# Loads of the start phase: all of X first, two weight tiles from ScalarE's queue, one split ahead of the lead, seven banks in turn

## The chip, the cores and the metric

The kernel runs on one core of one Trainium2 chip. The metric is the device time of one execution in microseconds. Five engines work side by side, each through its own instructions in order, and wait for each other by semaphores: TensorE (PE in the profile, its weight loads PEld), VectorE (DVE), ScalarE (ACT), GpSimd (POOL) and SyncE (SP). SP, ACT and POOL also issue the DMA transfers. The rows SPq and ACTq are those engines' queues: a DMA that stands there waiting holds up whatever stands behind it on the same engine.

## The reference

For x of 2048 rows and 576 columns there are two attentions of 32 heads of 18 columns each, one with its own keys and values per head (A) and one in which all heads share a key and a value (B), mixed by a gate.

```python
g = _sigmoid((x * gate_w).sum(-1, keepdims=True))
a = _A_ref(x, A_wqkv, A_wo)              # 32 heads: softmax(q k^T / sqrt(18)) v, then @ wo
b = _B_ref(x, B_wq, B_wk, B_wv, B_wo)    # the same, one k and one v for all heads
return g * a + (1 - g) * b
```

Everything is float32. The kernel forms most products from a rounded high part and a low part (h and l), three products of halves for each product.

## The kernel before

X is held transposed: 576 rows (the contraction, in five slabs of 128 with the last half full twice) by 2048 columns. All projection weights stand side by side in `wall`, cut into 14 tiles of 128 columns. Tile 0 holds B's shared key, the gate, B's shared value and the first queries. Tiles 0 to 4 are projected at the start and in the lead, the other nine later, in between the attention's own work.

The work runs in three stretches.

1. **The start phase** (to about 50 us). Tiles 0, 1 and 2 are projected for the four chunks of 512 columns of X. X's first chunk comes as two halves (`xsh`), the others as `xs`, numbered 2, 3 and 4 in the code's `load_x`. Each load is three DMAs: the main part of 128 partitions by `load5`, then the last 64 rows twice. Each chunk is cut into halves by `split_x`: ACT makes the high part `xh` (line 388), DVE the low part `xl` (394) and the last slab's low part (398). PE does 14 products per tile and chunk (line 278). `leave` takes the bank out of PSUM: ACT writes the high part of `phl` (284) and, for tile 0, a plain copy `pst` (287); DVE makes the low part (289); DMAs store them (`kq`, `qk`). `shared_v` then turns the value rows of `pst` round on PE (line 326), so PE waits there for ACT's copy. PE's order is fixed by the code: after tile 0 and tile 1 of the first chunk stand the four transposes of line 326, then tile 2, then the second chunk.
2. **The lead** (to about 91 us), whose order is written out as a string of letters. A and B are half-height products of tiles 3 and 4 (line 963), x and y are the first heads' score maxima (1115), taken out by ACT (1119, `xd`) and DVE (1125, `junk`).
3. **The main stretch**, in which scores, exponentials, maxima and the second products of all 64 heads alternate, ordered by strings and a small clock model. PE sets its pace to the end.

Banks of PSUM: seven are given out. In the start phase `Clock.turn` hands them out in fixed rings, ring "s" of three for projections and ring "m" of four for the warming products and `shared_v`. From the lead on, the bank that the model frees first is taken.

Queues: SP issues nearly all loads and the small stores of `kq`, ACT four loads at the very beginning, POOL a few loads and the large stores. The DMAs of SP and ACT share eight completion semaphores, called DMAHW0 to DMAHW7 in the built program, handed out in turn. Before a DMA takes a semaphore, its earlier user must have landed, and the issuing engine waits for that. `load_x(4)`, the last chunk of X, and the weights of tiles 3 and 4 are issued on SP behind the stores of the first chunk. Tile 3 is split (`prep_w`, lines 250 and 251) in the start phase, tile 4 inside the lead.

Of the kernel before, what the change touches and what calls it, by code (L numbers as in the profile page):

```python
# [8 lines left out]
F32 = mybir.dt.float32  # L9
# [19 lines left out]
NT = 5  # L29
# [18 lines left out]
class Clock:  # L48


    def __init__(self):
        self.free = [0.0] * 7
        self.t = self.act = self.dve = self.last = 0.0
        self.mode, self.begun, self.tail = "", [0.0, 0.0], [0.0, 0.0]
        self.turns, self.count, self.held, self.diffs, self.copies = {"s": 0, "m": 0}, 0, {}, [], []
        self.cleared, self.half = 0.0, HALF_MM

    def turn(self, which):
        n = self.turns[which]
        self.turns[which] += 1  # L60
        self.count += 1
        k = n % 3 if which == "s" else 3 + n % 4
        self.free[k] = -1e6 + self.count
        return k

# [91 lines left out]
def gated_mix_kernel(ctx: ExitStack, tc: tile.TileContext, xT, wall, wv, wo, out):  # L157
    nc = tc.nc
    P = 128

    def dma(o, i, eng=None):
        o, i = (x.bitcast(F32) if x.dtype == F32R else x for x in (o, i))
        return (eng or nc.sync).dma_start(o, i)  # L163
# [46 lines left out]
    def in_turn(which):  # L210
        return bank_tile(clk.turn(which))
# [24 lines left out]
    def split(src, h, l, eng_h, eng_l):  # L236
        if eng_h is nc.scalar:
            nc.scalar.activation(h, src, AF.Copy)
        else:
            eng_h.tensor_copy(h, src)  # L240
        if l is not None:
            eng_l.tensor_tensor(l, src, h.bitcast(F32), op=OP.subtract)

    def load5(t, src, rest=None):
        dma(t[:, 0:4, :], src[0:512, :].rearrange("(p k) m -> p k m", p=P))
        dma(t[0:64, 4, :], src[512:576, :], rest)
        dma(t[64:128, 4, :], src[512:576, :], rest)

# [1 line left out]
        nc.scalar.activation(w["h"], st, AF.Copy)  # L250
        eng_l.tensor_tensor(w["l"], st, w["h"].bitcast(F32), op=OP.subtract)

    def load_w(mt, rest=None):
        st = wpool.tile([P, NKT, P], F32, name="wst", bufs=5)
        load5(st, wall[mt], rest)
        return st

    def prep_w(st):
        w = {y: wpool.tile([P, NKT, P], F32R, name=f"w{y}", bufs=3) for y in "hl"}
        split_w(st, w, nc.vector)  # L260
        return w
# [4 lines left out]
    def project(mt, c, w, parts=1):  # L266


        fp = in_turn("s")
        g = 512 // parts  # L270
        for i in range(parts):
            products(fp, w, c * 512, g * i, g)
        return leave(mt, c, fp)
# [47 lines left out]
        return c, st  # L321

    def shared_v(c, st):
        pv = in_turn("m")
        for j in range(4):
            nc.tensor.transpose(pv[:, 18 * j:18 * j + 18],
                                st[ROW_VB:ROW_VB + 18, j * P:(j + 1) * P],
                                ident[ROW_VB:ROW_VB + 18, ROW_VB:ROW_VB + 18])
        nc.vector.tensor_copy(vb[:, 4 * c:4 * c + 4, 0:18],
                              pv[:, 0:72].rearrange("p (j d) -> p j d", d=18))  # L330
# [35 lines left out]
    with tc.tile_pool(name="xs", bufs=1, side="right") as xsp:  # L366
        XS = []

        def load_x(c, rest=None):
            half = c < 2  # L370
            XS.append(xsp.tile([P, NKT, 256 if half else 512], F32, name="xsh" if half else "xs", bufs=2 if half else 3))
            load5(XS[c], xT[:, 256 * c:256 * c + 256] if half else xT[:, 512 * (c - 1):512 * c], rest)

        def main_w(st):

            w = {y: wpool.tile([P, NKT, P], F32R, name=f"w{y}", bufs=3) for y in "hl"}
            nc.scalar.activation(w["h"][:, 0:4], st[:, 0:4], AF.Copy)
            nc.vector.tensor_tensor(w["l"][:, 0:4], st[:, 0:4], w["h"][:, 0:4].bitcast(F32), op=OP.subtract)
            return w

        def last_w(st, w):
            nc.scalar.activation(w["h"][:, 4], st[:, 4], AF.Copy)
            nc.vector.tensor_tensor(w["l"][:, 4], st[:, 4], w["h"][:, 4].bitcast(F32), op=OP.subtract)

        def split_x(c):
            xs = XS[c // 2 + 1][:, :, 256 * (c % 2):256 * (c % 2) + 256] if c > 1 else XS[c]
            cs = slice(c * 256, (c + 1) * 256)
            nc.scalar.activation(X["h"][:, :, cs], xs, AF.Copy)
            low_x(c, xs)
            last_x(c, xs)  # L390

        def low_x(c, xs):
            cs = slice(c * 256, (c + 1) * 256)
            nc.vector.tensor_tensor(X["l"][:, :, cs], xs[:, 0:4], X["h"][:, 0:4, cs].bitcast(F32), op=OP.subtract)

        def last_x(c, xs):
            xh = X["h"][64:128, 4, c * 256:(c + 1) * 256]
            nc.vector.tensor_tensor(xh, xs[64:128, 4], xh.bitcast(F32), op=OP.subtract)

        W = [load_w(0, nc.scalar)]  # L400
        load_x(0, nc.scalar)
        nc.scalar.activation(ones, ones, AF.Copy)
        W.append(load_w(1, nc.gpsimd))
        W.append(load_w(2, nc.gpsimd))
        load_x(1, nc.gpsimd)

        warm = in_turn("m")
        for i in range(6):
            nc.tensor.matmul(warm[:, 0:304], ident, vb.rearrange("p k d -> p (k d)"), start=True, stop=True)
        for c in range(2, 4):  # L410
            load_x(c)
        dma(ones_r.rearrange("a (b c) -> (a b) c", c=32), ones)

        x0, xh = XS[0], X["h"][:, :, 0:256]
        ST = [W.pop(0) for _ in range(3)]
        WP = [main_w(ST[0])]
        nc.scalar.activation(xh[:, 0:2], x0[:, 0:2], AF.Copy)
        nc.vector.tensor_copy(xh[:, 2:4], x0[:, 2:4])
        low_x(0, x0)
        WP.append(main_w(ST[1]))  # L420
        WP.append(main_w(ST[2]))
        last_w(ST[0], WP[0])
        nc.scalar.activation(xh[:, 4], x0[:, 4], AF.Copy)
        last_x(0, x0)
        last_w(ST[1], WP[1])
        last_w(ST[2], WP[2])
        split_x(1)
        FP = [in_turn("s") for _ in range(3)]
        for n in ((0, 12), (12, 14)):
            for mt in range(3):  # L430
                products(FP[mt], WP[mt], 0, 0, 256, *n)
        keep = []

        def chunk(c):
            split_x(2 * c)
            split_x(2 * c + 1)

        for mt in range(3):
            if mt == 2:
                chunk(1)  # L440
                shared_v(*keep.pop())
            products(FP[mt], WP[mt], 0, 256, 256)
            keep.append(leave(mt, 0, FP[mt]))
            keep = [k for k in keep if k]
            if mt == 0:
                load_x(4)
                for m in range(3, NT):
                    W.append(load_w(m))
        for n, (mt, c) in enumerate(FIRST):
            if n == 1:  # L450
                chunk(2)
            if n == 2:
                chunk(3)
            if keep and keep[0][0] <= n - 2:
                shared_v(*keep.pop(0)[1])
            done = project(mt, c, WP[mt], 2 if n == 0 else 1)
            if done:
                keep.append((n, done))
            if (mt, c) == (0, 2):
                first_back()  # L460
            if (mt, c) == (0, 3):
                rows_back()
            if n == 6:
                WP.append(prep_w(W.pop(0)))

    xdp = ph1.enter_context(tc.tile_pool(name="xdp", bufs=1, side="right"))
    small = ctx.enter_context(tc.tile_pool(name="small", bufs=1, side="left"))
# [619 lines left out]

    def lead_units():
        yield
        for mt in range(3, NT):  # L1090
            w = WP.pop()
            for c in range(4):
                if (mt, c) == (3, 1):
                    for _ in range(NT - 4):
                        WP.append(prep_w(W.pop(0)))
                st = stp.tile([P, 512], F32, name="pst", bufs=3)
                st2 = xdp.tile([P, 512], F32, name="pst2", bufs=2)

                def done(mt=mt, c=c, st=st, st2=st2):
                    hl = stp.tile([P, 2, 512], F32R, name="phl", bufs=4)  # L1100
                    nc.gpsimd.tensor_tensor(st, st, st2, op=OP.add)
                    split(st, hl[:, 0, :], hl[:, 1, :], nc.gpsimd, nc.gpsimd)
                    dma(qk_d[:, mt * P:(mt + 1) * P, c * 512:(c + 1) * 512].rearrange("a p f -> p a f"), hl,
                        nc.gpsimd)

                yield Unit([(w[a][:, k, :], X[b][:, k, c * 512:(c + 1) * 512]) for a, b, k, _ in PROJ],
                           512, (st, st2), done, how="both", upper=-1)

    def lead_max(what, low):
        M, h = pairs[what].pop(0)  # L1110
# [187 lines left out]
```

## Time and profile before

| what | value |
|---|---|
| median of three runs | 2636.14 us (2635.72 to 2636.35) |
| the profiled execution, its own time | 2633.82 us |
| its span, first to last instruction | 2632.0 us |
| PE busy | 2621.7 us, 100% of the span |
| ACT busy, DVE busy | 2447.6 us and 2395.4 us |
| granted TensorE clock, mean | 0.999 |
| start phase, PE's products of line 278 | 7.81 to 50.5 us |

A row of the timeline gives the start in us, the duration, the engine, the line, the operation with output<-input, the number of instructions merged, and in brackets the idle time before it and what ended that. The chain of work that ended last gives start, duration and the work or transfer that held the end. PE's busy time is modelled and says little about how full it is; the chain and the gaps say more.

### The profile page before, as it was taken

The numbers are of one execution on the slowest core, as the hardware profiler recorded it, in microseconds if no ns is written. First come the engines' busy times: TensorE is split into PE (matmuls) and PEld (weight loads), VectorE is DVE, ScalarE is ACT, GpSimd is POOL, SyncE is SP. The second block draws the span as 40 slices with busy tenths as digits, with TensorE's granted clock in tenths as the row PEclk, the third lists the DMA queues.
The fourth block names the chain that finished last, engine by engine and source line by source line (L and its number), as shares of the span: only waits on it lengthen the run. The fifth ranks groups of instructions, "written<-read, shape, count | busy, mean of one in ns | idle before, by whom it ended". The sixth has DMA issues, their size and how long they took to land.

```text
span 2632.0 us, 66889 instructions
## 1 busy us (share of the span) xinstructions
PE 2621.7 (100%) x25213; PEld 1404.5 (53%) x25213; DVE 2395.4 (91%) x4575; ACT 2447.6 (93%) x4862; POOL 850.5 (32%) x1087
## 2 busy tenths in 40 slices
PE   9999999999999999999999999999999999999999
PEld 7655545545455455554554555545555544545665
DVE  6899999999999999999999999999998999999883
ACT  5999999999999999999999999999999999999887
POOL 3611000211364535644554446443310020012113
PEclk9999999999999999999999999999999999999999
DMA  8412112212343234323544344434432332234312
GB/s 259 140 54 62 36 48 59 75 48 74 96 123 105 91 97 120 113 89 93 152 130 137 119 138 141 142 118 121 141 95 76 101 98 85 61 88 126 110 56 92
DMA packets 176328, 270.28 MB, mean 103 GB/s; under 512 B 58905, under 2 KB 137193, under 8 KB 164625
## 3 DMA queue, kind: packets, MB, share of 16 engines
q1 hardware_dynamic: 159813, 212.70, 28.2%
q0 software_dynamic: 15152, 51.79, 5.3%
q8 instruction: 198, 3.24, 0.5%
q10 hardware_dynamic: 1040, 1.52, 0.2%
q14 instruction: 125, 1.02, 0.1%
HBM read 190.26 MB, written 66.90 MB: 98 GB/s over the span
## 4 chain that ended last, share of the span: by engine, by line
PE 98%; DMA 1%; DVE 0%; ACT 0%; SPq 0%; POOL 0%; issue 0%; ACTq 0%; DVEq 0%
PE acc L755 39%; PE bank L695 29%; PE bank L740 17%; PE bank L963 11%; PE bank L278 1%; PE bank L1115 0%; PE bank L943 0%; DMA xsh<-xT 0%; PE acc L767 0%; DMA R<-r_d 0%; SPq L163 0%; POOL oacc L936 0%; DMA wst<-wall 0%; PE bank L1017 0%; DMA sm<-sum_d 0%
## 5 line engine op out<-in xcount | busy, mean ns | idle before, releaser
L748 ACT ACTIVATE pt<-bank 128x512 f32<-128x512 f32 x4096 | 2146.4, 616 | 120.4 <-PE bank L740 68.7
L704 DVE TENSOR_REDUCE mx<-bank 128x1 f32<-128x512 f32 x3002 | 1886.9, 684 | 118.2 <-PE bank L740 60.3
L740 PE MATMUL bank<-qs,ksb 56*128 56x512 f32 x2688 | 906.8, 424 | 0.0
L695 PE MATMUL bank<-ksb,qs 54*128 54x512 f32 x2270 | 806.4, 426 | 0.0
L755 PE MATMUL acc<-pt,vb 128*19 128x256 f32 (+3 forms) x6144 | 553.2, 455 | 0.0
L695 PEld LDWEIGHTS bank<-ksb,qs 54*128 54x128 f32 x2270 | 382.8, 184 | 318.8 <-ACT pt L748 190.3
L755 PE MATMUL acc<-pt,vg 128*19 128x512 f32 (+3 forms) x5952 | 535.0, 455 | 0.0
L740 PEld LDWEIGHTS bank<-qs,ksb 56*128 56x128 f32 x2688 | 441.1, 184 | 153.9 <-DVE mx L704 63.8
L740 PE MATMUL bank<-qs,ksa 56*128 56x512 f32 x1408 | 466.6, 425 | 0.0
L695 PE MATMUL bank<-ksa,qs 54*128 54x512 f32 x1232 | 439.2, 426 | 0.0
L701 DVE CUSTOM_DVE_ANT_0 junk<-bank,xb 128x512 bf16<-128x512 f32 x500 | 342.9, 686 | 29.4 <-PE bank L740 23.6
L698 ACT ACTIVATE xb<-bank 128x512 f32<-128x512 f32 x500 | 292.6, 606 | 13.7 <-PE bank L740 3.2
L695 PEld LDWEIGHTS bank<-ksa,qs 54*128 54x128 f32 x1232 | 207.8, 184 | 151.1 <-ACT pt L748 87.4
L240 POOL CAST mh<-mt 128x32 fp32r<-128x32 f32 x62 | 13.0, 210 | 831.1 <-DVE mt L713 608.8
L740 PEld LDWEIGHTS bank<-qs,ksa 56*128 56x128 f32 x1408 | 225.5, 184 | 84.2 <-DVE mx L704 31.3
L755 PEld LDWEIGHTS acc<-pt,vb 128*19 128x19 f32 x6144 | 123.1, 97 | 203.1 <-issue 169.6
L755 PEld LDWEIGHTS acc<-pt,vg 128*19 128x19 f32 x5952 | 119.7, 97 | 206.2 <-issue 180.2
L240 POOL CAST rhl<-rst 128x292 fp32r<-128x292 f32 (+2 forms) x81 | 34.0, 420 | 486.7 <-issue 316.4
L963 PE MATMUL bank<-xr,wrh 64*128 64x292 f32 (+1 forms) x1134 | 167.9, 300 | 0.0
L695 PE MATMUL bank<-kdb,qs 54*128 54x512 f32 x372 | 159.8, 430 | 0.0
L963 PEld LDWEIGHTS bank<-xr,wrh 64*128 64x128 f32 x1134 | 139.5, 186 | 2.8
L558 POOL TENSOR_TENSOR xr<-xst,xr 128x876 fp32r<-128x876 f32 (+1 forms) x63 | 130.4, 2070 | 0.0
(171 smaller groups left out, 2397.0 us busy)
## 6 DMA issues: line engine op xcount, KB each, us to landing
qs<-qk SPq DMA_DIRECT2D x366, 144.0 KB
xst<-xT SPq DMA_DIRECT2D x54, 438.0 KB
ksa<-qk SPq DMA_DIRECT2D x132, 144.0 KB
qk<-rhl POOLq DMA_DIRECT2D x54, 292.0 KB, 4.3
ksb<-qk SPq DMA_DIRECT2D x60, 144.0 KB
qk<-phl POOLq DMA_DIRECT2D x16, 512.0 KB, 5.4
onh<-oh POOLq DMA_DIRECT2D x32, 256.0 KB, 3.9
onl<-ol POOLq DMA_DIRECT2D x32, 256.0 KB, 4.7
```

What stands on the lines that cost most here:

```text
L240: eng_h.tensor_copy(h, src)
L278: nc.tensor.matmul(fp[:, p0:p0 + g], w[a][:kr, k, :], X[b][:kr, k, x0 + p0:x0 + p0 + g], start=(n == 0), stop=(n == len(PROJ) - 1))
L558: nc.gpsimd.tensor_tensor(x[:, 5:8, 0:n], t0, x[:, 0:3, 0:n].bitcast(F32), op=OP.subtract)
L695: nc.tensor.matmul(pm, qs[u % 3][b:b + 54, i * P:(i + 1) * P], k, start=True, stop=True)
L698: nc.scalar.activation(MX["x", u, i], pm, AF.Relu)
L701: nc.vector.tensor_tensor_reduce(junk, pm, MX.pop(("x", u, i)), 1.0, -3e38, op0=OP.add, op1=OP.max, accum_out=MX[u][:, i, c:c + 1])
L704: nc.vector.tensor_reduce(MX[u][:, i, c:c + 1], pm, axis=AX.X, op=OP.max)
L740: nc.tensor.matmul(ps, kst(u)[b:b + 56, i * P:(i + 1) * P], qs[u % 3][b:b + 56, c * 512:(c + 1) * 512], start=True, stop=True)
L748: nc.scalar.activation(pt, ps, AF.Exp, scale=SCALE)
L755: nc.tensor.matmul(acc[32 * j:32 * j + 19, a:b], v_of(u, i), PT[u, i, j][:, a:b], start=(i == 0), stop=(i == 15), skip_group_check=True)
L963: nc.tensor.matmul(u.fp[op][:, 0:u.n], x[b:b + 64], y[b:b + 64], start=(n == 0), stop=(n == last))
```

## The change

Four things are rearranged in the start phase; no arithmetic changes.

- `load_x(4)` is issued with the others at the beginning, ahead of the store of `ones_r`. On SP it no longer stands behind the stores of the first chunk.
- The weights of tiles 3 and 4 are issued by ACT, all six DMAs, right behind `split_x(1)` and so ahead of the first `leave`. Before, SP issued them behind `load_x(4)`.
- Tile 4's split (`prep_w`) moves out of the lead to the eighth group of `FIRST`. `first_back`, the fetch of the first rows of keys and queries, follows the group (2, 1) in place of (0, 2).
- `project`, `shared_v` and the three first banks take all seven banks in one ring "g".

```diff
-        k = n % 3 if which == "s" else 3 + n % 4
+        k = n % 3 if which == "s" else 3 + n % 4 if which == "m" else n % 7
...
-    def load5(t, src, rest=None):
-        dma(t[:, 0:4, :], src[0:512, :].rearrange("(p k) m -> p k m", p=P))
+    def load5(t, src, rest=None, main=None):
+        dma(t[:, 0:4, :], src[0:512, :].rearrange("(p k) m -> p k m", p=P), main)
         dma(t[0:64, 4, :], src[512:576, :], rest)
         dma(t[64:128, 4, :], src[512:576, :], rest)
...
-        fp = in_turn("s")
+        fp = in_turn("g")
...
-        pv = in_turn("m")
+        pv = in_turn("g")
...
-        for c in range(2, 4):
+        for c in range(2, 5):
             load_x(c)
         dma(ones_r.rearrange("a (b c) -> (a b) c", c=32), ones)
...
         split_x(1)
-        FP = [in_turn("s") for _ in range(3)]
+        W = [load_w(m, nc.scalar, nc.scalar) for m in range(3, NT)]
+        FP = [in_turn("g") for _ in range(3)]
...
-            if mt == 0:
-                load_x(4)
-                for m in range(3, NT):
-                    W.append(load_w(m))
...
-            if (mt, c) == (0, 2):
+            if (mt, c) == (2, 1):
                 first_back()
...
-            if n == 6:
+            if n in (6, 7):
                 WP.append(prep_w(W.pop(0)))
...
-                if (mt, c) == (3, 1):
-                    for _ in range(NT - 4):
-                        WP.append(prep_w(W.pop(0)))
```

On ACT, between the split of the second half chunk (`xsh`) and the split of chunk 2 (`xs`), there stood before, with the semaphores that each row waits for (`wst` is a weight tile as loaded, DMAHW and DMASW are completions of DMAs of SP or ACT and of POOL):

```order
L388 ACTIVATE xh<-xsh 128x5x256 [waits DMAHW0_49,DMASW5_49,DMASW4_49]
L284 ACTIVATE phl<-bank_181 128x512 [waits PE_49]
L287 ACTIVATE pst<-bank_181 128x512
L284 ACTIVATE phl<-bank_182 128x512 [waits PE_49]
L388 ACTIVATE xh<-xs 128x5x256 [waits DMAHW3_49,DMAHW2_49,DMAHW1_49]
L388 ACTIVATE xh<-xs 128x5x256
```

and now, at the same place on ACT:

```order
L388 ACTIVATE xh<-xsh 128x5x256 [waits DMAHW0_49,DMASW5_49,DMASW4_49]
L163 DMA wst<-wall 128x512
L163 DMA wst<-wall 64x128
L163 DMA wst<-wall 64x128 [waits DMAHW1_49]
L163 DMA wst<-wall 128x512 [waits DMAHW3_49]
L163 DMA wst<-wall 64x128 [waits DMAHW4_49]
L163 DMA wst<-wall 64x128 [waits DMAHW5_49]
L284 ACTIVATE phl<-bank_193 128x512 [waits PE_49]
L287 ACTIVATE pst<-bank_193 128x512
L284 ACTIVATE phl<-bank_194 128x512 [waits PE_49]
L388 ACTIVATE xh<-xs 128x5x256 [waits DMAHW2_49]
L388 ACTIVATE xh<-xs 128x5x256
```

Six DMAs, four of them with a wait, now stand between the split and the first `leave`.

On SP, from the main part of chunk 2 on (a DMA that waits for a DMAHW semaphore is its next user), there stood before:

```order
L163 DMA xs<-xT 128x4x512 [waits DMAHW1_49]
L163 DMA xs<-xT 64x512 [waits DMAHW2_49]
L163 DMA xs<-xT 64x512 [waits DMAHW3_49]
L163 DMA xs<-xT 128x4x512 [waits DMAHW4_49]
L163 DMA xs<-xT 64x512 [waits DMAHW5_49]
L163 DMA xs<-xT 64x512 [waits DMAHW6_49]
L163 DMA ones_r<-ones 128x32 [waits DMAHW7_49,Activation_49]
L163 DMA kq<-phl 54x2x512 [waits DMAHW0_49,DVE_49]
L163 DMA kq<-phl 54x512 [waits DMAHW1_49]
L163 DMA kq<-phl 18x2x512 [waits DMAHW2_49]
L163 DMA kq<-phl 18x512 [waits DMAHW3_49]
L163 DMA z_d<-pst 1x512 [waits DMAHW4_49,Activation_49]
```

and now:

```order
L163 DMA xs<-xT 128x4x512 [waits DMAHW1_49]
L163 DMA xs<-xT 64x512 [waits DMAHW2_49]
L163 DMA xs<-xT 64x512 [waits DMAHW3_49]
L163 DMA xs<-xT 128x4x512 [waits DMAHW4_49]
L163 DMA xs<-xT 64x512 [waits DMAHW6_49]
L163 DMA xs<-xT 64x512 [waits DMAHW0_49]
L163 DMA xs<-xT 128x4x512 [waits DMAHW2_49]
L163 DMA xs<-xT 64x512 [waits DMAHW6_49]
L163 DMA xs<-xT 64x512 [waits DMAHW7_49]
L163 DMA ones_r<-ones 128x32 [waits DMAHW0_49,Activation_49]
L163 DMA kq<-phl 54x2x512 [waits DMAHW1_49,DVE_49]
L163 DMA kq<-phl 54x512 [waits DMAHW2_49]
```

Chunk 4 has moved up, chunks 2 and 3 stand as before, and the main parts of chunks 2 and 3 still take DMAHW1 and DMAHW4, for which ACT's third and fifth DMA wait next.

More of the change, by code (lines that the diff above doesn't have):

```diff
@@ L54, in __init__ @@
         self.mode, self.begun, self.tail = "", [0.0, 0.0], [0.0, 0.0]
-        self.turns, self.count, self.held, self.diffs, self.copies = {"s": 0, "m": 0}, 0, {}, [], []
+        self.turns, self.count, self.held, self.diffs, self.copies = {"s": 0, "m": 0, "g": 0}, 0, {}, [], []
         self.cleared, self.half = 0.0, HALF_MM
@@ L251, in split_w, with load_w @@
         eng_l.tensor_tensor(w["l"], st, w["h"].bitcast(F32), op=OP.subtract)
-    def load_w(mt, rest=None):
+    def load_w(mt, rest=None, main=None):
         st = wpool.tile([P, NKT, P], F32, name="wst", bufs=5)
-        load5(st, wall[mt], rest)
+        load5(st, wall[mt], rest, main)
         return st
@@ L462, in gated_mix_kernel @@
                 rows_back()
-            if n == 6:
+            if n in (6, 7):
                 WP.append(prep_w(W.pop(0)))
+        while keep:
+            shared_v(*keep.pop(0)[1])
     xdp = ph1.enter_context(tc.tile_pool(name="xdp", bufs=1, side="right"))
@@ L1089, in lead_units, with done @@
         yield
-        for mt in range(3, NT):
-            w = WP.pop()
-            for c in range(4):
-                if (mt, c) == (3, 1):
-                    for _ in range(NT - 4):
-                        WP.append(prep_w(W.pop(0)))
[L1096 to L1107, printed above, removed]
+        for mt, c in [(mt, c) for mt in range(3, NT) for c in range(4)]:
+            w = WP[mt]
+            st = stp.tile([P, 512], F32, name="pst", bufs=3)
+            st2 = xdp.tile([P, 512], F32, name="pst2", bufs=2)
+            def done(mt=mt, c=c, st=st, st2=st2):
+                hl = stp.tile([P, 2, 512], F32R, name="phl", bufs=4)
+                nc.gpsimd.tensor_tensor(st, st, st2, op=OP.add)
+                split(st, hl[:, 0, :], hl[:, 1, :], nc.gpsimd, nc.gpsimd)
+                dma(qk_d[:, mt * P:(mt + 1) * P, c * 512:(c + 1) * 512].rearrange("a p f -> p a f"), hl, nc.gpsimd)
+            yield Unit([(w[a][:, k, :], X[b][:, k, c * 512:(c + 1) * 512]) for a, b, k, _ in PROJ],
+                       512, (st, st2), done, how="both", upper=-1)
     def lead_max(what, low):
```

## The prediction

> **What bounds the kernel now.** I read the chain of work that ended last first, for the whole span and then for the start phase, since only that phase and the head of the lead are rearranged.
>
> ```profile
> PE 98%; DMA 1%; DVE 0%; ACT 0%; SPq 0%; POOL 0%; issue 0%; ACTq 0%; DVEq 0%
> ```
>
> ```profile
> 13.57 1.22 PE bank L278 x8
> ...
> 17.84 8.65 PE bank L278 x56
> ...
> 26.84 9.88 PE bank L278 x42
> ...
> 40.83 9.77 PE bank L278 x42
> ```
>
> PE holds the end nearly everywhere, and from 13.57 us to the lead its products follow each other. Nothing ahead of PE is worth time here unless it stops PE; and a stop of PE is not made good, it moves everything behind it. So the question is which stops go and which come. How near PE is to a stop just there is seen in the timelines of ACT, DVE and PE:
>
> ```profile
> 12.25 1.27 ACT L388 ACTIVATE xh<-xsh 128x1280 fp32r<-128x1280 f32 x1 [1.57 <-DMA xsh<-xT]
> 15.85 0.60 ACT L284 ACTIVATE phl<-bank 128x512 fp32r<-128x512 f32 x1 [2.33 <-PE bank L278]
> 16.35 0.59 ACT L287 ACTIVATE pst<-bank 128x512 f32<-128x512 f32 x1
> ...
> 18.02 2.42 ACT L388 ACTIVATE xh<-xs 128x1280 fp32r<-128x1280 f32 x2
> ```
>
> ```profile
> 22.29 0.42 DVE L398 TENSOR_TENSOR xh<-xs,xh 64x256 fp32r<-64x256 f32 x1
> ```
>
> ```profile
> 17.42 0.42 PE L326 MATMUL bank<-ident,pst 18*128 18x18 f32 x4
> ...
> 22.89 0.28 PE L278 MATMUL bank<-xh,wh 128*128 128x256 f32 x1
> ```
>
> ACT's copy `pst` ends at 16.94, half a microsecond before PE's transposes (line 326) need it. The split of chunk 2 ends on DVE at 22.71, and PE uses its last slab in the products that end the group, at 22.77 and 22.89. ACT, DVE and PE run here in step: a later ACT is a later PE.
>
> **The change part by part.**
>
> *Six DMAs on ACT.* ACT reaches them at 13.52 (12.25 + 1.27). Its own issues at the beginning, and what SP did later, give the price:
>
> ```profile
> 0.75 1.19 ACTq L163 DMA_DIRECT2D wst<-wall  x2
> 1.97 1.49 ACTq L163 DMA_DIRECT2D xsh<-xT  x2
> 3.49 1.28 ACT L402 ACT_TABLE_LOAD   x1 [3.49 <-issue]
> ```
>
> ```profile
> 17.69 2.40 SPq L163 DMA_DIRECT2D kq<-phl  x4
> 20.60 0.23 SPq L163 DMA_DIRECT2D z_d<-pst  x1
> ```
>
> ```profile
> SPq L163 <- DMA xs<-xT: 0.5, 1, 0.5
> ```
>
> One issue holds ACT 0.60 (1.19 / 2) to 0.75 us, and ACT's first work came only behind its four. The larger price is a wait. The fifth of the six waits for DMAHW4, whose user ahead of it is the main part of X's chunk 3. In the profile the store `z_d` waits for the same semaphore and transfer: the stores ahead of it end at 20.09, it stands 0.5 us (the wait above) and goes at 20.60. So chunk 3's main part landed at about 20.55. In the changed kernel ACT cannot pass its fifth DMA before that, and the first `leave`, free at 15.85 now, stands behind it.
>
> It will land later still. The weights of tiles 3 and 4 move beside it; sizes from the list of DMAs, the rate from the stretch ahead of that landing (the last two numbers are the busy share of the DMA engines and GB/s):
>
> ```profile
> wst<-wall SPq DMA_DIRECT2D x5, 256.0 KB
> wst<-wall SPq DMA_DIRECT2D x4, 32.0 KB
> ```
>
> ```profile
> 14.00:16.00 2.00, 1.96 (x16) 1.75 (x15) 1.20 (x2) 0.15 (x1) 0.00 (x0) 1.00 1.06 248
> ```
>
> The DMA engines are full. Ahead of the wait ACT has issued tile 3 whole (320 KB) and tile 4's main part (256 KB), 590,000 bytes in all: between nothing and 2.4 us (590 / 248). I take 1.45 us, all of tile 3 (1.3) and a little of tile 4, which is issued late since it waits for chunk 2 first. Chunk 3 lands at 22.0 (20.55 to 22.95). Two issues follow, 1.2 us (1.1 to 1.7), so the first `leave` starts at T = 23.2 (21.65 to 24.65).
>
> On the rate a page speaks against the change: by the Trainium skill, DMA: Bandwidth & Descriptors, section Issuing engines are not separate DMA queues, transfers from SP, ACT and GpSimd run on the same 16 engines and a second issuing engine saves only issue time. By it all bytes count, the 2.4 us end, and the sum would be 0.95 us larger; no row shows the two queues side by side on full engines.
>
> What that does to PE: from T, `phl`, `pst` and the second `phl` follow at the pitch of 0.5 us seen above (15.85 to 16.35), PE having long ended both groups, and the split of chunk 2 starts at T + 1.5. It took from 18.02 to 22.71, 4.69 us, so it ends at T + 6.2 against 22.71: PE is later by T - 16.5 = **6.7 us** (5.15 to 8.15). PE stands still from 17.42 to about T + 1.15 = 24.35.
>
> *The clock behind that stop.* The only long stillness of PE in the trace is its end:
>
> ```profile
> 2626.11 0.29 PE L943 MATMUL bank<-wol,qs 128*128 128x288 f32 x1
> ```
>
> ```profile
> 2628.00:2630.00 2.00, 0.00 (x0) 0.00 (x0) 0.00 (x0) 0.00 (x0) 0.00 (x0) 0.62 0.91 325
> 2630.00:2632.00 2.00, 0.00 (x0) 0.00 (x0) 0.00 (x0) 0.00 (x0) 0.00 (x0) 0.50 0.01 3
> ```
>
> A granted mean of 0.62 over two microseconds is 1.0 for 0.48 us and 0.5 after, so the clock halved at 2628.5, 2.1 us behind the last product. A stop of 7 us should do the same. How long it then stays halved no row shows; the nearest is the warming stretch, which kept one pace throughout:
>
> ```profile
> 1.93 5.84 PE L409 MATMUL bank<-vb,ident 128*128 128x304 f32 x12 [1.93 <-DVE ones L200]
> ```
>
> Half a clock for 0 to 5.84 us costs 0 to 2.9 us, PE having 5.7 us of products in step there (17.42 to 23.1). I take **2.5 us**, near the upper end, since the stop is three times the 2.1. The Trainium skill, TensorE: Matmul & The Clock Gate, section Part 1: The HAM clock gate (the "warmup" mystery), gives one idle window of about 3.4 us for the fall and a busy one for the return, in windows that run freely: estimated from it, 3.4 to 6.8 us at half, 1.7 to 3.4 us. The trace agrees with the fall; the return no run shows yet.
>
> *Tile 4's split out of the lead.* ACT, then DVE:
>
> ```profile
> 55.77 0.75 ACT L250 ACTIVATE wh<-wst 128x640 fp32r<-128x640 f32 x1
> 56.39 0.61 ACT L1119 ACTIVATE xd<-bank 128x512 f32<-128x512 f32 x1
> ```
>
> ```profile
> 57.29 0.68 DVE L1125 CUSTOM_DVE_ANT_0 junk<-bank,xd 128x512 bf16<-128x512 f32 x1
> ```
>
> ```profile
> 58.04 0.49 PE L1115 MATMUL bank<-ksb,qs 54*128 54x512 f32 x1 [0.49 <-DVE mx L1125]
> ```
>
> Without it `xd` starts at 55.77 and ends at 56.38, `junk` follows then and not at 57.29, and PE's product at 58.04, which waits for `junk`, comes up to 0.9 us sooner. Below, 0, if a bank holds PE instead. I take **0.8 us gained**. In the start phase the split stands behind the (1, 3) group, where ACT idles:
>
> ```profile
> 50.63 0.60 ACT L284 ACTIVATE phl<-bank 128x512 fp32r<-128x512 f32 x1 [2.52 <-PE bank L278]
> ```
>
> 2.52 us of idleness cover its 0.75; without that cover it would cost those.
>
> *Chunk 4 at the beginning.* ACT's split of it waited, and PE did not:
>
> ```profile
> 30.74 2.44 ACT L388 ACTIVATE xh<-xs 128x1280 fp32r<-128x1280 f32 x2 [3.52 <-DMA xs<-xT]
> ```
>
> PE's chain runs unbroken from 26.84 for 9.88 us across it. Gain 0. Behind it on SP stand `ones_r` and the stores of the first chunk, now held until chunk 3's last rows land; their `phl` comes late with T anyway, so no cost.
>
> *Seven banks, first rows sooner.* Between 23 and 50.4 us PE's weight loads waited for nothing but this:
>
> ```profile
> PEld bank L326 <- issue: 1.1, 3, 0.4
> PEld bank L278 <- ACT xh L388: 0.2, 1, 0.2
> ```
>
> No wait for a bank: gain 0. `first_back` makes SP wait for the `kd` stores earlier, with the stores of chunk 2 behind it. The tightest use of what follows on SP is `keb` in the lead:
>
> ```profile
> 52.52 0.26 SPq L163 DMA_DIRECT2D keb<-ke  x1
> ```
>
> ```profile
> 58.86 0.39 PE L1115 MATMUL bank<-keb,qs 54*128 54x512 f32 x1
> ```
>
> Cost 0 while those 6 us of room last; without them, each microsecond of delay on SP is one on PE.
>
> **Sum:** 6.7 + 2.5 - 0.8 = +8.4 us (4.25 to 11.05 from the bounds). On the profiled execution's 2633.82 that is 2642.2; the runs' median lies 2.3 us above it, so on the median **2644.5 us**, from 2640.4 to 2647.2.
>
> **The rivals.**
>
> *The clock stays full.* Stop as forecast, no halved stretch: 6.7 - 0.8 = +5.9, 2642.0. For it, no long stop stands inside the kernel; against it, the fall 2.1 us behind the last product.
>
> *ACT is not held, and the time does not grow.* If chunk 3's main part lands before ACT asks, six issues of 0.6 us from 13.52 end at 17.1, PE loses 17.1 - 16.5 = 0.6 and wins 0.8: 2635.9, no change. It decides from a landing at about 16 us on. Against it: `z_d` found it missing at 20.09, and the changed kernel puts more beside it.
>
> *A late queue behind the stop.* If SP, waiting for `kd`, brings `keb` or chunk 4 late, the lead or the (0, 3) group stops too: the 6 us of room must go, and each microsecond beyond adds one; four make 2648.5.
>
> **How the numbers follow.** Forecast 0.66, clock full 0.20, ACT not held 0.07, late queue 0.07. A measurement of this kernel tells about 0.2%, 5.3 us, from no change, so 2641.4 is the border. Of the forecast's chance 0.63 lie above it, of the clock's rival 0.12, of the late queue's all: slower 0.82, within 0.16, faster 0.02 (it would need 5.3 us of gain where the only stop removed is worth 0.9). The range 2640.0 to 2647.5 holds the bounds of the sum and the rival clock, and leaves out ACT not held and most of the late queue.
>
> **What would show it.** Right: ACT's six DMAs from 13.5 to about 23, `phl` first at about 23 and not 15.85; PE's transposes at about 24.4; a granted clock below 1 between 20 and 30 us; line 278 ending near 60 and not 50.5; no line 250 or 251 in the lead. Wrong: `phl` still near 17, or PE's delay at the lead's start being less than at 25 us, which would mean slack that the chain does not show.

## The result, and the profile after

| kernel | median of the timed runs | lowest to highest, runs |
|---|---|---|
| before | 2636.11 us | 2634.36 to 2638.33, 14 |
| changed | 2641.81 us | 2639.70 to 2643.53, 14 |

The ratio is 1.0022, with a 95% interval from 1.0015 to 1.0029: slower by 5.7 us, with the whole interval above 1. The forecast was 2644.5. The profiled execution of the changed kernel took 2643.53 us, 9.7 us more than that of before. That pair exaggerates: before's 2633.82 lies below the whole range of its 14 timed runs, and the 2643.53 is the top of its own range.

The timeline of ACT in the changed kernel (start, duration, engine, line, operation, count, and in brackets the idle time ahead and what ended it) shows where the time goes:

```profile
12.84 1.27 ACT L388 ACTIVATE xh<-xsh 128x1280 fp32r<-128x1280 f32 x1 [2.50 <-DMA xsh<-xT]
12.86 11.09 ACTq L163 DMA_DIRECT2D wst<-wall  x6
23.99 0.60 ACT L284 ACTIVATE phl<-bank 128x512 fp32r<-128x512 f32 x1 [9.89 <-DMA wst<-wall]
24.49 0.59 ACT L287 ACTIVATE pst<-bank 128x512 f32<-128x512 f32 x1
```

The six DMAs stand in ACT's queue until 23.95, and the first `leave`, at 15.85 before, starts at 23.99. ACT computed nothing for 9.89 us. In shorter windows of the same view the last four of the six come as two pairs:

```profile
16.49 1.74 ACTq L163 DMA_DIRECT2D wst<-wall  x2
22.82 1.12 ACTq L163 DMA_DIRECT2D wst<-wall  x2
```

Between the pairs, from 18.23 to 22.82, the queue stood for 4.6 us. In this trace the completion events of chunk 3's main part end at 22.80, and the fifth DMA goes at 22.82. PE's timeline of the same stretch:

```profile
17.80 0.28 PE L278 MATMUL bank<-xh,wl 128*128 128x256 f32 x1
25.13 0.61 PE L326 MATMUL bank<-ident,pst 18*128 18x18 f32 x4 [7.06 <-ACT pst L287]
25.67 1.22 PE L278 MATMUL bank<-xh,wh 128*128 128x256 f32 x4
26.69 1.05 PE L278 MATMUL bank<-xh,wl 128*128 128x256 f32 x4
...
30.22 0.64 PE L278 MATMUL bank<-xl,wh 128*128 128x256 f32 x4
```

PE ends its two groups at 18.08, stands 7.06 us for ACT's `pst`, and begins again at a slow pace: a group of four 256-column products takes 1.22 and 1.05 us at first and 0.64 us from 30.22 on. The table by stretches (busy time of PE, PEld, DVE, ACT and POOL, then the granted clock) says why:

```profile
20.00:22.00 2.00, 0.00 (x0) 0.00 (x0) 0.00 (x0) 0.00 (x0) 0.00 (x0) 1.00 1.08 253
22.00:24.00 2.00, 0.00 (x0) 0.00 (x0) 0.00 (x0) 0.01 (x1) 0.00 (x0) 0.74 1.05 308
...
26.00:28.00 2.00, 2.00 (x11) 2.00 (x11) 1.62 (x2) 1.88 (x2) 1.40 (x2) 0.50 0.77 199
28.00:30.00 2.00, 2.00 (x12) 2.00 (x12) 1.93 (x3) 0.60 (x1) 0.00 (x0) 0.55 0.92 310
30.00:32.00 2.00, 2.00 (x19) 2.00 (x18) 1.07 (x3) 0.00 (x0) 0.56 (x1) 1.00 0.40 141
```

A mean of 0.74 means that the clock fell at 22.97, and 0.55 that it came back at 29.8: 6.83 us at half. The chain of work that ended last runs, in the start phase, through exactly this stop:

```profile
17.89 6.12 DMA wst<-wall
24.01 0.58 ACT phl L284
24.59 0.50 ACT pst L287
...
25.13 0.61 PE bank L326 x4
25.74 10.24 PE bank L278 x56
...
50.22 9.77 PE bank L278 x42
59.98 1.59 PE bank L962 x12
```

The row `wst<-wall` is an inference of the chain: it starts at 17.89, where ACT issued tile 4's main part, but the first `leave` waits for no DMA of its own, only for PE and for what stands ahead of it in ACT's queue. There the last long wait is the one for chunk 3.

The lead begins at 59.98; before, the last line-278 stretch ended at 50.60 (40.83 + 9.77). So the start phase is 9.4 us longer in this pair of profiles. In the lead some of it comes back: measured at the same instructions of ACT, the distance to before is 8.15 us from 75 to 109 us. Then, at about 120 us, it grows to 10.0 and stays between 9.6 and 10.3 to the end. That second step is not the change's doing, as the experiments show; it stands at this row of DVE (line 240, the rounded high part of head 1's negated row maxima):

```profile
122.12 1.90 DVE L240 CAST mh<-mt 128x32 fp32r<-128x32 f32 x1
124.05 0.58 DVE L242 TENSOR_TENSOR mh<-mt,mh 128x32 fp32r<-128x32 f32 x1
```

In before's profile the same cast took:

```profile
113.97 0.29 DVE L240 CAST mh<-mt 128x32 fp32r<-128x32 f32 x1
```

### The profile page after: what moved, and what is told of

It reads as the page before. It is cut to its first block, busy times and chain, and to the rows that moved or that the text cites. A ratio compares the mean times of both kernels' runs of the same rounds, so it can differ in the third digit from the quotient of the medians.

```text
span 2641.7 us, 66891 instructions
## 1 busy us (share of the span) xinstructions
PE 2622.7 (99%) x25213; PEld 1407.0 (53%) x25213; DVE 2397.3 (91%) x4575; ACT 2446.8 (93%) x4862; POOL 850.5 (32%) x1087
## 4 chain that ended last, share of the span: by engine, by line
PE 98%; DMA 1%; DVE 0%; ACT 0%; POOL 0%; issue 0%; ACTq 0%; SPq 0%; DVEq 0%
PE acc L754 38%; PE bank L694 29%; PE bank L739 17%; PE bank L962 11%; PE bank L278 1%; PE acc L766 1%; PE bank L942 1%; DMA wst<-wall 0%; PE bank L1109 0%; DMA xs<-xT 0%; POOL oacc L935 0%; DVE mx L703 0%; DVE mh L240 0%; PE bank L1016 0%; PE bank L326 0%
```

## The experiments

My theory: the six DMAs hold ACT until chunk 3's main part has landed, this stops PE, and the stop halves the clock; everything else is worth under 2 us. Rivals: chunk 4's earlier load, not ACT, delays things; the issues themselves cost, not the wait; the clock costs nothing. Each kernel was timed against the kernel before on the same chip; a difference below is taken from the runs of before in its own group (medians 2635.33, 2635.85, 2635.79 and 2636.06). The intervals of the ratios reach 2 to 3 us to either side, so a difference of 1 or 2 us between medians is weak by itself and needs its rows beside it.

### The weights back on SP

The changed kernel, with

```diff
-        W = [load_w(m, nc.scalar, nc.scalar) for m in range(3, NT)]
+        W = [load_w(m) for m in range(3, NT)]
```

> The changed kernel with one word undone: the six weight loads of tiles 3 and 4 are issued by SP, at the same place in the program, in place of ACT. Theory (ACT is held behind its fifth DMA until chunk 3 lands): the first leave starts at about 16 us as before, PE does not stop, the clock stays at 1.00, and what is left is the gain in the lead, about 1 us: 2635 us. Rival (the cost comes from seven banks, the earlier fetch of the first rows or chunk 4 at the beginning, all of which stay): 2641 to 2642 us as with the whole change.

Measured: 2634.24 us (2633.00 to 2636.62), ratio 0.9996 [0.9987, 1.0005]. ACT's first `leave`, and the start of the lead in the chain:

```profile
15.62 0.60 ACT L284 ACTIVATE phl<-bank 128x512 fp32r<-128x512 f32 x1 [2.33 <-PE bank L278]
```

```profile
50.27 2.05 PE bank L962 x14
```

Both are where they stood before, and the clock is full. So the engine that issues the weights is the whole loss. What is left of the change costs nothing, and perhaps gains a microsecond.

### The weights on ACT, and nothing else

The kernel before, with the `W = [...]` line of the change behind `split_x(1)` and without its two weight loads on SP; chunk 4 and the split stay as before.

> The kernel before with that one part alone: the weights of tiles 3 and 4 issued by ACT behind the split of the second half chunk, all else as before. Theory: ACT is held as in the changed kernel, the first leave starts at 23 to 24 us, PE stops for about 7 us and runs at half clock for some microseconds, no gain in the lead: 2642 to 2644 us. Rival (the DMAs on ACT are harmless alone and only chunk 4 in front of them makes them late): the first leave before 19 us, within 2 us of 2636.

Measured: 2642.72 us (2640.00 to 2646.45), ratio 1.0027 [1.0016, 1.0037].

```profile
12.40 10.61 ACTq L163 DMA_DIRECT2D wst<-wall  x6
23.05 0.60 ACT L284 ACTIVATE phl<-bank 128x512 fp32r<-128x512 f32 x1 [9.40 <-DMA wst<-wall]
```

```profile
8.22 13.64 DMA xs<-xT
```

The whole stop is there with chunk 4 still late. Chunk 4's early load is not its cause. Here the chain runs through chunk 3's load itself, to 21.86, and on through ACT's last two issues to `phl`.

### Tile 4's split alone

The kernel before, with the split moved:

```diff
-            if n == 6:
+            if n in (6, 7):
                 WP.append(prep_w(W.pop(0)))
...
-                if (mt, c) == (3, 1):
-                    for _ in range(NT - 4):
-                        WP.append(prep_w(W.pop(0)))
```

> The kernel before with tile 4's split moved out of the lead alone. Theory: the lead is 0.8 to 1.3 us shorter and nothing else moves: 2635 us. Rival (another wait takes the place of the split, the lead keeps its length): 2636.1 us, and the lead's first 10 us as long as before.

Measured: 2635.12 us (2633.16 to 2637.45), ratio 0.9998 [0.9989, 1.0007]: by time no difference that can be told. In its profile the distance to before falls by 0.97 us in the head of the lead. The start ahead of it was 0.85 us later, about half a microsecond of that because PE waited for chunk 4:

```profile
26.13 6.57 DMA wst<-wall
32.74 1.26 ACT xh L388
34.05 3.52 PE bank L278 x14
```

The chain passes through ACT's split of chunk 4, which stands here behind the stores and the weights on SP. In the three other profiled executions with the late load and without the stop (before twice, and before with short pieces, below) PE did not stand there. So the early load of chunk 4 is worth something in some executions at most.

### The six DMAs one chunk later

The changed kernel, with the `W = [...]` line moved behind `chunk(1)`, so that the first two `leave`s and chunk 2's split stand ahead of the six DMAs on ACT.

> The changed kernel with the same six DMAs on ACT, but behind the split of chunk 2 in place of the split of the second half chunk. They now wait for still later transfers (the last rows of chunk 3, the main part of chunk 4), but nothing that PE needs soon stands behind them on ACT. Theory (it is what stands behind the wait that costs, not the wait): ACT is held for some microseconds from about 20 us, PE goes on, 2635 to 2636 us. Rival (ACT's issuing or the shared DMA engines cost the time): 2640 us or more.

Measured: 2643.47 us (2641.17 to 2644.54), ratio 1.0028 [1.0017, 1.0040]. A miss: the theory had 2635 to 2636.

```profile
21.95 8.11 ACTq L163 DMA_DIRECT2D wst<-wall  x6
30.11 1.08 ACT L284 ACTIVATE phl<-bank 128x512 fp32r<-128x512 f32 x2 [9.87 <-DMA wst<-wall]
```

```profile
31.73 0.61 PE L326 MATMUL bank<-ident,pst 18*128 18x18 f32 x4 [5.46 <-ACT pst L287]
```

```profile
17.48 10.95 DMA kq<-phl
```

With another place in the order the DMAs got other semaphores. By the trace the first two waited as expected, for chunk 3's last rows and for chunk 4's main part, and the second went at 25.58. But four more stood behind it, and the last two, which in the changed kernel had waited for chunk 3's main part and for tile 3's own first load, now waited for `kq` stores of the first chunk; the chain shows such a store under way from 17.48 to 28.43. The six held ACT's queue for 8.1 us. The expectation failed in holding that nothing PE needs soon stands behind them: ACT's next `pst` does. PE stopped for 5.46 us, and the clock halved for 6.83. Which transfers the moved DMAs will wait for has to be read from the new program, for all six.

### Warming products in the stop

The changed kernel, with 13 more products of `ident` and `vb` into a bank that nobody reads, behind tile 1's group and ahead of the transposes:

```diff
+        def keep_warm(n):
+            wb = in_turn("m")
+            for _ in range(n):
+                nc.tensor.matmul(wb[:, 0:304], ident, vb.rearrange("p k d -> p (k d)"), start=True, stop=True)
...
+                keep_warm(13)
```

> The changed kernel with 13 warming products (the form of the very first ones, result unused) on PE between tile 1's group and the transposes for which PE stops: 26 instructions of 0.25 us at full clock, 6.6 us, about the length of the stop. Theory: the first leave stays at 23 to 24 us, PE is now busy until then, the clock stays at 1.00 between 18 and 30 us, and the lead starts 2.3 us sooner than in the changed kernel (half of the 4.66 us that PE worked at half clock): about 2639.5 us. Rival (behind the stop ACT and DVE set the pace, and half the clock costs nothing): the lead starts within 0.5 us of 59.98 and the time stays at 2641.8 us.

Measured: 2639.80 us (2638.92 to 2641.68), ratio 1.0014 [1.0005, 1.0023], so 2.0 us less than the changed kernel, or 1.75 if each is set against its own group's runs of before.

```profile
17.67 6.81 PE L438 MATMUL bank<-vb,ident 128*128 128x304 f32 x26
24.42 0.42 PE L326 MATMUL bank<-ident,pst 18*128 18x18 f32 x4
24.77 0.74 PE L278 MATMUL bank<-xh,wh 128*128 128x256 f32 x4
```

```profile
57.28 1.59 PE bank L968 x11
```

The added products fill the stop, the granted clock is 1.00 from 18 to 26 us, and PE goes on at full pace (0.74 us, where the changed kernel took 1.22). By times alone the 2 us are not clear of noise, since the two intervals overlap. In the profiles the lead starts 2.7 us sooner (57.28 against 59.98), of which 0.7 us are there already at the transposes (24.42 against 25.13), because ACT came free sooner. The other 2.0 us are what the halved clock costs.

### Tile 3 on ACT, tile 4 on SP

```diff
-        W = [load_w(m, nc.scalar, nc.scalar) for m in range(3, NT)]
+        W = [load_w(3, nc.scalar, nc.scalar), load_w(4)]
```

> The changed kernel with tile 3's three loads on ACT and tile 4's three on SP, at the same place. The last wait on ACT is now for chunk 2's main part, which lands near 16.5 us, and no longer for chunk 3. Theory (the wait for chunk 3 is the cost): ACT is free at about 17.1 us, PE is 0.6 to 1.2 us late, the lead gives 1.2 back: 2635 to 2636 us. Rival (every DMA on ACT costs alike, by its issue or by its bytes): half of the stop remains, 2638 us or more.

Measured: 2635.00 us (2633.03 to 2637.97), ratio 0.9997 [0.9988, 1.0006].

```profile
12.04 3.99 ACTq L163 DMA_DIRECT2D wst<-wall  x3
16.08 0.60 ACT L284 ACTIVATE phl<-bank 128x512 fp32r<-128x512 f32 x1 [2.79 <-PE bank L278]
```

Three issues, with one wait among them, hold ACT 3.99 us and end as PE's products do. They cost nothing there; the price lies with tile 4's three, and above all with the wait for chunk 3.

### Both kernels once more, for their spread

The changed kernel and the kernel before, each with a comment line at its head, so that its line numbers stand one higher; one execution each.

> The changed kernel once more, for a second profile. Theory (the 2 us that the profile lost behind 115 us at DVE's CAST of mh are chance, the stop at the start is not): the first leave at 23 to 24 us again, PE's first product of the lead at 59.5 to 60.5 us, while the CAST of mh behind 115 us takes anything from 0.3 to 2 us. Rival (the change moved POOL's work onto that CAST): it takes 1.9 us again, and 0.3 in the kernel before.

> The kernel before once more, for a second profile, as the counterpart of the last run. Theory: PE's first product of the lead at 50.3 to 51.5 us again, the CAST of mh behind 107 us takes anything from 0.3 to 2 us and the whole lies 0 to 3 us above the first profile. Rival: 0.3 us again and 2633.8 us.

Measured: 2645.01 and 2637.15 us. The changed kernel's stop had another size, PE first and then the clock:

```profile
24.54 0.61 PE L327 MATMUL bank<-ident,pst 18*128 18x18 f32 x4 [6.68 <-ACT pst L288]
```

```profile
20.00:22.00 2.00, 0.00 (x0) 0.00 (x0) 0.00 (x0) 0.00 (x0) 0.00 (x0) 0.63 1.11 225
30.00:32.00 2.00, 2.00 (x16) 2.00 (x16) 0.55 (x1) 0.00 (x0) 0.73 (x1) 0.81 0.23 77
```

The stop is shorter by 0.4 us, but the clock fell earlier, at 20.5, and came back at 30.76: 10.24 us at half, 6.2 of them under PE's work, 3.1 us lost. From this pair of profiles the difference is 7.83 us at 109 us and 8.1 at the end; from the first pair it was 8.15 and 10.0. The first pair's extra 2 us are thus chance. In this execution of the changed kernel the cast of line 240 (241 here) took 1.73 us, and in that of before 1.56. The row of POOL beside the latter tells what it met:

```profile
114.37 1.56 DVE L241 CAST mh<-mt 128x32 fp32r<-128x32 f32 x1
115.96 0.58 DVE L243 TENSOR_TENSOR mh<-mt,mh 128x32 fp32r<-128x32 f32 x1
```

```profile
113.84 2.04 POOL L243 TENSOR_TENSOR vwl<-wvs,vwh 128x864 fp32r<-128x864 f32 x1
115.84 0.65 POOL L241 CAST vwh<-wvs 128x576 fp32r<-128x576 f32 x1
```

DVE's cast ends at 115.93, 0.05 us behind POOL's 115.88, and its subtraction at 116.54, 0.05 us behind POOL's next one. In the changed kernel's profile the cast ends at 124.02 and POOL's subtraction at 123.98:

```profile
121.94 2.04 POOL L242 TENSOR_TENSOR vwl<-wvs,vwh 128x864 fp32r<-128x864 f32 x1
```

Behind this wait PE stood 0.93 us in the second execution of before, and the clock was at half from 118.7 to 122.1, both of which the first profile of before lacked.

### GpSimd's splits in short pieces, and with them a better version

The edit in all three kernels, of the split of the value weights:

```diff
-                split(t, w[hf]["h"][:, k0:k1], w[hf]["l"][:, k0:k1], nc.gpsimd, nc.gpsimd)
+                for k in range(k0, k1):
+                    split(t[:, k - k0], w[hf]["h"][:, k], w[hf]["l"][:, k], nc.gpsimd, nc.gpsimd)
```

On the changed kernel with the weights on SP:

> The changed kernel with the weights of tiles 3 and 4 on SP again, and GpSimd's splits of the value weights cut into pieces of 288 columns in place of 864 and 576 (five casts of about 0.3 us and five subtractions of about 0.7 us for each half, in place of 0.90, 2.04, 0.66 and 1.42). Theory (VectorE's small cast of the row maxima of head 1 can't run while GpSimd holds an instruction that reads and writes SBUF, and waits to its end): the cast at about 113 us waits for one short piece, so 0.3 to 1.0 us in place of 0.75 to 1.95, its subtraction 0.2 to 0.8; it never meets a piece of 2 us. TensorE's stop there is short, the clock stays full, and the time lies 0.5 to 2 us under that of the same kernel with the long pieces (2634.24): 2632.2 to 2633.8, below the kernel before by 1.5 to 3 us. Rival (the cast's length has another cause, such as the sequence on VectorE): the cast still takes 1.5 to 2 us in most executions, and the time stays at 2634 to 2635. Second rival: with short pieces GpSimd always has another one ready, and VectorE loses to each in turn, so that cast and subtraction together take as long as before.

On the kernel before:

> The kernel before with that edit of GpSimd's splits alone, nothing else changed. Theory (the same): 0.5 to 2 us under the kernel before, 2633.5 to 2635.3, since its profiled executions had casts of 0.29 and 1.56 us; the spread of its runs shrinks from about 4 us to about 3. Rival: 2635 to 2636, no difference.

On the changed kernel as it is, and once more the first:

> The changed kernel, weights of tiles 3 and 4 on ACT as in it, with GpSimd's splits of the value weights cut into pieces of 288 columns. In the traces the changed kernel stands 7.8 to 8.2 us behind the kernel before at 106 us, ahead of the place where VectorE's cast meets GpSimd, and by the times only 5.7. Theory A (the missing 2 us are chance at that place, where the kernel before loses more in its usual execution than the changed kernel does): with the place taken out of both the difference is that of the traces, so this kernel lies 7 to 8.5 us above the kernel before with the same short pieces (2634.8): 2641.8 to 2643.3, no faster than the changed kernel. Theory B (the place costs both alike, and the start is dearer by 2 us in profiled executions than in others): 5 to 6.5 us above it, 2639.8 to 2641.3. The clock halves at about 22 us as before in both.

> Again the changed kernel with the weights on SP and GpSimd's splits in pieces of 288 columns, for its time alone: 2632.5 to 2634, ratio to the kernel before 0.998 to 1.000. If its first result was chance, 2634 to 2635 and no difference.

| kernel with short pieces | median | lowest to highest, runs | ratio to before |
|---|---|---|---|
| changed, weights on SP | 2633.01 us | 2632.28 to 2636.37, 11 | 0.9990 [0.9981, 0.9998] |
| the same again | 2633.36 us | 2632.73 to 2633.63, 11 | 0.9990 [0.9981, 0.9998] |
| before | 2634.80 us | 2633.70 to 2635.53, 11 | 0.9996 [0.9987, 1.0005] |
| changed | 2640.91 us | 2639.76 to 2642.74, 11 | 1.0019 [1.0010, 1.0028] |

In the first of them DVE and POOL met again, for a shorter time:

```profile
112.75 0.39 DVE L240 CAST mh<-mt 128x32 fp32r<-128x32 f32 x1
113.17 0.34 DVE L242 TENSOR_TENSOR mh<-mt,mh 128x32 fp32r<-128x32 f32 x1
```

```profile
112.30 0.80 POOL L242 TENSOR_TENSOR vwl<-wvs,vwh 128x288 fp32r<-128x288 f32 x1
113.04 0.42 POOL L240 CAST vwh<-wvs 128x288 fp32r<-128x288 f32 x1
```

The cast ends at 113.14, the piece at 113.10. The waits follow POOL's instruction, whatever its length, so the cause of the second step is shown. The Trainium skill, SBUF — State Buffer, section SBUF: two separate sides, has this: VectorE and GpSimd share a port pair, the one that starts first holds it for its whole instruction, and the other waits; of VectorE's instructions this holds for those in a mode that uses both ports and, against a GpSimd instruction that reads SBUF, for those with two inputs in SBUF. The rows agree, with 0.03 to 0.05 us from the one's end to the other's. In which mode the cast ran no run shows.

The changed kernel with the weights on SP and short pieces beats both kernels, that of before by 2.8 and 2.7 us in two groups, each time with an interval that ends just below 1. By itself neither part reaches a difference that can be told from zero (0.9996 each).

The fourth kernel bears on two readings of the missing 2 us (8 us in the profiles, 5.7 by time). With the place at 115 us mended in both, the two stand 6.1 us apart by their medians (5.8 when each is set against its own runs of before), while their profiled executions stand 8.05 us apart at 109 us and 7.8 at the end. By its median the expectation's second theory (5 to 6.5 us) held, which speaks against the meeting of DVE and POOL as the place of the missing 2 us. It does not settle it: the interval of the ratio spans 2.6 to 7.4 us and leaves room for the first theory. The second theory's words go too far as well. The profiled execution of before with short pieces took 2633.82 us, 0.98 below its median, and that of the changed kernel 2641.39, 0.48 above: their difference is 7.57, and 1.46 of it is where these two single executions lie in their ranges. In the usual execution the kernel before loses about a microsecond more, and the changed kernel about half a microsecond less, than the profiles show. Where, the runs did not show.

## Why the prediction came out so

The time lay in the range, and slower was likeliest; the forecast's sum was 2.7 us too large. Its terms, as the profiles and, where a pair of kernels isolates them, the times give them:

| term | predicted | in profiles | by times |
|---|---|---|---|
| stop on PE | 6.7 (5.15 to 8.15) | 7.7 and 6.6 | 4.8 to 5.8 |
| halved clock behind it | 2.5 (0 to 2.9) | 2.3 and 3.1 | 1.75 to 2.0 |
| both together | 9.2 | 9.4 and 8.9 | 6.8 to 7.55 |
| the rest: split out of the lead, chunk 4, banks, first rows | -0.8 | -0.8 to -1.2 | -1.1 to -1.8 |
| sum | +8.4 | +7.8 to +10.0 | +5.7 |

The profile values of the stop are the shift of PE's transposes, 25.13 against 17.42 and, in the second pair, 24.54 against 17.90. "Both together" is the changed kernel against the same with the weights on SP. With the long pieces it stands 5.70 us above its own runs of before, the other 1.09 below, 6.8 in all. With short pieces it is 4.85 above against 2.70 below, 7.55; the weights on ACT alone cost 7.4. The stop by times is this less the clock's 1.75 to 2.0. In the profiles with short pieces the two stand 8.05 and 0.81 us on the two sides of before, 8.9 in all; the 9.4 is the shift of the lead's start in the first pair. "The rest" is the kernel with the weights on SP against before: 1.09 with long pieces, 2.70 - 0.99 and 2633.01 against 2634.80 with short ones.

*The wait on ACT.* Right in kind: the six DMAs held ACT from 12.86 to 23.95 (forecast 13.5 to about 23). The completion events of chunk 3's main part end at 22.80 in the changed kernel's trace, where I had 22.0, and 21.87 in the kernel with the weights on ACT alone; the first `leave` followed the landing by 1.19 us, where I had 1.2. `leave` began at 23.05, 23.24, 23.41, 23.64 and 23.99 in five executions with these DMAs, so the landing varies by about a microsecond, as much as the two ways of counting tile 4's bytes differed (0.95). By the rule of the Trainium skill, DMA: Bandwidth & Descriptors, section Issuing engines are not separate DMA queues, all bytes count, and the forecast's estimate for that was 22.95; the 22.80 lies near it, the 21.87 does not, and the runs don't decide it.

*That a later ACT is a later PE.* Right: the transposes moved as `pst` did, and the lag remained to the lead.

*The clock.* Right: it halved, and putting products into the stop took 2 us away. The estimate's upper end was too low for one execution, in which the clock stayed at half for 10.24 us and cost 3.1.

*Tile 4's split.* Right in kind, and low: the distance falls by 1.24 us in the head of the lead (9.39 to 8.15), and by 1.25 and 1.28 in the two pairs with short pieces, where I had 0.8 and an upper end of 0.9. Alone on the kernel before it was 0.97. I had counted only the one `xd` behind the split; in the changed kernel PE waits for no maximum at all in that stretch.

*Chunk 4 early, 0.* Perhaps low. PE waited half a microsecond for chunk 4 in one of four executions with the late load, and by times the rest of the change gains 1.1 to 1.8 us, of which the split alone is about 1.2. Chunk 4's load was not tested by itself.

*Seven banks and first rows, 0.* No wait of PE for a bank or for `keb` appears in the changed kernel's head of the lead. They were not timed alone.

The mechanism held, and what was off is a size, the sum: 8.4 us forecast, 5.7 by times. The largest part of it lies in "PE is later by T - 16.5 = 6.7 us", which by times is worth 4.8 to 5.8. That term was sized on one profiled execution, and in the profiles it held (7.7 and 6.6 us, and 8.15 and 7.83 for the whole at 109 us). So the step that does not carry over is the one from a profiled execution to the median of the runs. The intervals of the ratios are about as wide as the gap, and which part of the stop the usual execution is spared stays open. Of the rivals, the full clock named nearly the right time (2642.0) for a wrong reason: the kernel with its clock kept full ran at 2639.8.

## What to carry to other kernels

Before a DMA is moved to an engine that also computes, look up which transfer its completion semaphore belonged to last, in the new order, and when that lands: of the 11.1 us for which the six DMAs held ACT's queue the issues took 3.0 (0.34 to 0.70 each) and the waits 8.1. A stop of PE cost its length and then about 2 us of slow clock behind it, so a stop of this length that cannot be removed is worth filling. Compare several profiled executions before explaining a step of 2 us, and set the sum against times, not against one pair of profiles.

## What the runs showed of the hardware

The half clock lasted 3.41, 6.83 or 10.24 us, one, two or three times 3.413, and it began anywhere from 2.7 us (at 20.52, last product ended at 17.86) to 4.9 us (at 22.97, against 18.08) behind the last product. The Trainium skill, TensorE: Matmul & The Clock Gate, section Part 1: The HAM clock gate (the "warmup" mystery), has a freely running window of 3413 ns; all lengths agree with it. It has the fall behind at least one idle window, and with that the falls after 2.1 us (end of the kernel) and 2.7 us agree less well, being shorter than one; the prediction's remark that the trace agrees with the fall was too kind.

Much shorter stops of PE were enough too. Behind the cast near 115 us PE stood 0.93 to 1.33 us in four profiled executions (both kernels repeated, the split alone, the DMAs one chunk later), and each time the clock then halved for one such stretch. In the changed kernel's first execution PE stood 1.27 us there and the clock stayed full. In the repeated execution of before it fell at 118.7:

```profile
116.00:118.00 2.00, 1.07 (x6) 0.50 (x5) 2.00 (x4) 1.15 (x3) 1.92 (x3) 1.00 0.08 16
118.00:120.00 2.00, 2.00 (x19) 0.62 (x17) 1.64 (x4) 1.36 (x3) 1.92 (x3) 0.68 0.03 4
120.00:122.00 2.00, 2.00 (x14) 0.99 (x14) 1.06 (x2) 1.04 (x3) 0.72 (x2) 0.50 0.53 150
```

A cast of 128x32 on DVE, 0.18 us at the least, took up to 1.95 us beside an instruction of 2.04 us on POOL. With such instructions cut short, the timed runs of before spread over 1.8 us (3.9 to 5.4 in its groups with long ones, of more runs). Those of the changed kernel with the weights on SP spread over 4.1 us in one group, 1.3 without its one slowest run, and over 0.9 in the other, against 3.6 with long ones. That the spread shrinks is thus likely, but not shown by every group.
